# Alpha for two chunks in one transfer, two positions on a partition, in a gated linear attention with a multiplicative feed-forward

## The chip, the cores and the metric

The kernel runs on one core of a Trainium2 chip. The metric is the device time of one execution in microseconds (us); the figure used is the median of several executions. The profile is of one further execution, and its span is a little different from the median. Engines are named as in the profile: PE is TensorE's matmul, PEld its weight load, DVE is VectorE, ACT ScalarE, POOL GpSimd, SP SyncE; a name with q at its end is that engine's own queue, for instance SPq, the SyncE queue that issues most of the DMA transfers.

## What is computed

A recurrence over 768 positions for 4 x 8 heads of 48 columns, and a feed-forward block on its output. All products have to be close to float32.

```python
def _attn_ref(q, k, v, alpha):                 # (4, 8, 768, 48) each, float32
    for t in range(S):
        state = alpha[:, :, t, :, None] * state + einsum('bhd,bhde->bhde' of k, v: outer product)
        y[:, :, t] = np.einsum('bhd,bhde->bhe', q[:, :, t], state)

# bridge: (B,H,S,D) -> x of (B*S, H*D) = (3072, 384)
def _moe_ref(x, w1, w2, w3, w_out):            # weights arrive as float64
    a = x @ w1                                 # 384 x 1024
    b = x @ w2
    h = a * b @ w3                             # 1024 x 1024
    return (h @ w_out).astype(np.float32)      # 1024 x 384
```

alpha lies between 0.8 and 1.0. (The einsum of the state is written here in words; the whole is the outer product of k and v at each position.)

## The kernel before

The positions are cut in chunks of C = 128, six to a batch, N = 24 in all. Within a chunk the recurrence becomes a masked matrix product: with the running sum of log(alpha) over the chunk's positions, k is multiplied by exp(-sum) and q by exp(sum); then scores = k q, masked, times v, plus the state of the chunks before. Two neighbouring chunks (n even, n + 1) share a point of reference, so an even chunk's sums run to its end and an odd one's from its start. The running sum is a product with a triangle of ones.

One chunk of alpha comes as 128 positions on 128 partitions, with 8 heads of 48 values each, and so in pieces of 48 values:

```python
    def rows(src, n):
        b, c = divmod(n, NCH)
        return src[b, :, ds(c * C, C), :].rearrange("h p d -> p h d")

    def load_a(n):
        if n < N:
            st["a", n] = inp.tile([C, H, D], FP32, tag="ac", name="ac")
            nc.sync.dma_start(out=st["a", n], in_=rows(alpha, n))           # L124
    # load_kq(n): k and q in the same way (L130, L131); load_v(n): v (L136)

    nc.scalar.preload_act_table_set(LN_EXP_SET)
    load_a(0)
    load_kq(0)
    load_a(1)
    load_v(0)
    load_kq(1)
    load_a(2)
    # ... constants: utri (ones on and above the diagonal), after = utri - 1,
    #     sums: both as fp32r
```

The logarithms, the sums and the exponentials. The first ten chunks use float32 products; from LATE = 10 on the logarithms are split in two fp32r parts:

```python
    def logs(n):
        a = st.pop(("a", n)).rearrange("p h d -> p (h d)")
        la = st["la", n] = work.tile([C, DM], FP32, tag="la", name="la")
        nc.scalar.activation(la, a, AF.Ln)                                  # L246
        if n >= LATE:
            t = st["la", n] = work.tile([C, 2, DM], FP32R, tag="la2", name="la2", bufs=1)
            nc.scalar.copy(t[:, 0], la)                                     # L250
            nc.vector.tensor_sub(t[:, 1], la, t[:, 0].bitcast(FP32))        # L251
        if n in ends:
            nc.gpsimd.dma_start(out=ends[n][2:3], in_=a[0:1])

    def decays(n):
        lc = bank()[:, 0:DM]                                                # one of 8 PSUM banks
        la = st.pop(("la", n))
        if n < LATE:
            nc.tensor.matmul(lc, utri if n % 2 else after, la, start=True, stop=True)     # L261
        else:
            for i in range(2):
                nc.tensor.matmul(lc, sums[:, n % 2], la[:, i], start=(i == 0), stop=(i == 1))  # L264
        e = st["e", n] = work.tile([C, 2, DM], FP32, tag="e", name="e", bufs=3)
        nc.scalar.activation(e[:, 0], lc, AF.Exp, scale=-1.0)               # L267
        nc.scalar.activation(e[:, 1], lc, AF.Exp)                           # L268
        if n in ends:
            nc.gpsimd.dma_start(out=ends[n][0:1], in_=e[0:1, 0])            # L270
        if n + 1 in ends:
            nc.gpsimd.dma_start(out=ends[n + 1][1:2], in_=e[C - 1:C, 1])    # L272
        load_ends(n)      # ends back from DRAM, one value to a partition, as dec (L285)

    def decayed(n):       # k and q times their exponentials
        nc.vector.tensor_mul(qks[n % 3][:, :, :, 0:D], st.pop(("kq", n)), ...)    # L277
```

What follows for a chunk: `transposed` (L299 on TensorE, copied out at L301), `scores` (L339, masked at L342), `outer` (L311), `advance` (the state times dec, L328 to L330, on GpSimd), `attend_state` (L358) and `attend` (L364, copied out at L368 and stored to DRAM by L236). Beside this the kernel converts the float64 weights (loads L181, ScalarE L189, L194, L207, VectorE L190 to L210, in steps called `convert`), and runs a part of the feed-forward's first two products as `gate` pieces (TensorE L396 and L400, emptied at L398 and L401). A gate product takes three fp32r parts of each operand, so that the result is as good as float32.

The order of the work:

```python
    logs(0)
    decays(0)
    decayed(0)
    transposed(0)
    logs(1)
    decays(1)
    convert(1, 1)
    load_v(1)
    load_kq(2)
    load_a(3)
    # ... decayed(1), further loads, load_a(4)

    for n in range(N + 1):
        store()
        load_v(n + AHEAD - 1)
        load_a(n + 5)
        load_kq(n + AHEAD)
        # attend_state(n - 1), scores(n), transposed(n + 1), split_x
        pieces = (0, 3, 3, 2)[(n - 6) % 4] if n > 5 else 0
        if n == 0:
            logs(2)
            decays(2)
            logs(3)
        # convert, advance(n), attend(n - 1), outer(n)
        run(pieces > 0)                     # gate pieces
        decayed(n + 2)
        logs(n + 4)
        # load_x, convert
        run(pieces > 1)
        decays(n + 3)
        # convert
        run(pieces > 2)
```

After the loop come the rest of the weights, w3 and w_out folded to one matrix (L439, L445), the other gate products, and the last product with the folded matrix (L396 and L400 with other tiles).

Of the kernel before, what the change touches and what calls it, by code (L numbers as in the profile page):

```python
# [10 lines left out]
FP32 = mybir.dt.float32  # L11
FP32R = mybir.dt.float32r
# [3 lines left out]
AF = mybir.ActivationFunctionType  # L16
ALU = mybir.AluOpType
# [31 lines left out]
def kernel(  # L49
# [12 lines left out]
    nc = tc.nc  # L62
    B, H, S, D = q.shape
    C = 128
    DM = H * D
    DF = moe_w1.shape[1]
    NCH = S // C
    N = B * NCH
    NP = H // 2
    DP = 64  # L70
# [7 lines left out]
    LATE = 10  # L78
# [3 lines left out]
    def pool(name, bufs, stack=ctx, **kw):  # L82
        return stack.enter_context(tc.tile_pool(name=name, bufs=bufs, **kw))
# [13 lines left out]
    p1 = pool("p1", 1, stack=part1, side="right", reuse_waits="tile")  # L97
    inp = pool("inp", 3, stack=part1, side="right", reuse_waits="tile")
    work = pool("work", 2, stack=part1, side="right", reuse_waits="tile")

    def bank():
        return ps.tile([C, 512], FP32, tag="bank", name="bank")

    st = {}
# [4 lines left out]
    ends = {n: dram.tile([3, DM], FP32, name=f"ends{n}") for n in range(2, N, 2) if n % NCH}  # L109
# [7 lines left out]
    def rows(src, n):  # L117
        b, c = divmod(n, NCH)
        return src[b, :, ds(c * C, C), :].rearrange("h p d -> p h d")

    def load_a(n):
        if n < N:
            st["a", n] = inp.tile([C, H, D], FP32, tag="ac", name="ac")
            nc.sync.dma_start(out=st["a", n], in_=rows(alpha, n))  # L124

    def load_kq(n):
        if n >= N:
            return
        st["kq", n] = inp.tile([C, 2, H, D], FP32, tag="kq", name="kq")
        nc.sync.dma_start(out=st["kq", n][:, 0], in_=rows(k, n))  # L130
        nc.sync.dma_start(out=st["kq", n][:, 1], in_=rows(q, n))  # L131

    def load_v(n):
        if n < N:
            st["v", n] = vs[n % len(vs)]
            nc.sync.dma_start(out=st["v", n][:, :, 0:D], in_=rows(v, n))  # L136

    nc.scalar.preload_act_table_set(LN_EXP_SET)
    load_a(0)
    load_kq(0)  # L140
    load_a(1)
    load_v(0)
    load_kq(1)
    load_a(2)
# [4 lines left out]

    w12 = const.tile([C, 3, 2, KM, DF], FP32R, name="w12")  # L150

    utri = p1.tile([C, C], FP32, name="utri")
    after = p1.tile([C, C], FP32, name="after")

    sums = p1.tile([C, 2, C], FP32R, name="sums")
    keep = p1.tile([C, C], I32, name="keep")
# [1 line left out]
    Ts = [p1.tile([C, NP, DP], FP32, name=f"T{i}") for i in range(2)]  # L158
    decs = [p1.tile([C, 3, NP], FP32, name=f"dec{i}") for i in range(2)]

    make_upper_triangular(nc, utri, val=1.0, diag=True)

    nc.vector.tensor_scalar_add(after, utri, -1.0)
    nc.gpsimd.tensor_copy(out=sums[:, 0], in_=after)
    nc.gpsimd.tensor_copy(out=sums[:, 1], in_=utri)
    nc.vector.memset(rebias, -(1023.0 - 127.0) * 2.0 ** 23)

    nc.vector.tensor_scalar_mul(keep, utri, -1.0)
# [45 lines left out]
    def convert(steps, ahead=3):  # L214

        for _ in range(steps):
            while weights and len(begun) < ahead:
                begun.append(weights.popleft())
                next(begun[-1])
            if not begun:  # L220
                return
            x = begun.popleft()
            try:
                next(x)
                begun.appendleft(x)
            except StopIteration:
                pass
# [4 lines left out]
    def store():  # L232

        while later:
            dst, src = later.popleft()
            nc.sync.dma_start(out=dst, in_=src)  # L236
# [1 line left out]
    def last(n):  # L238
        return n % NCH == NCH - 1

    def logs(n):
        if n >= N:
            return
        a = st.pop(("a", n)).rearrange("p h d -> p (h d)")
        la = st["la", n] = work.tile([C, DM], FP32, tag="la", name="la")
        nc.scalar.activation(la, a, AF.Ln)  # L246
        if n >= LATE:

            t = st["la", n] = work.tile([C, 2, DM], FP32R, tag="la2", name="la2", bufs=1)
            nc.scalar.copy(t[:, 0], la)  # L250
            nc.vector.tensor_sub(t[:, 1], la, t[:, 0].bitcast(FP32))  # L251
        if n in ends:
            nc.gpsimd.dma_start(out=ends[n][2:3], in_=a[0:1])

    def decays(n):
        if n >= N:
            return
        lc = bank()[:, 0:DM]
        la = st.pop(("la", n))
        if n < LATE:  # L260
            nc.tensor.matmul(lc, utri if n % 2 else after, la, start=True, stop=True)  # L261
        else:
            for i in range(2):
                nc.tensor.matmul(lc, sums[:, n % 2], la[:, i], start=(i == 0), stop=(i == 1))  # L264

        e = st["e", n] = work.tile([C, 2, DM], FP32, tag="e", name="e", bufs=3)
        nc.scalar.activation(e[:, 0], lc, AF.Exp, scale=-1.0)  # L267
        nc.scalar.activation(e[:, 1], lc, AF.Exp)  # L268
        if n in ends:
            nc.gpsimd.dma_start(out=ends[n][0:1], in_=e[0:1, 0])  # L270
        if n + 1 in ends:
            nc.gpsimd.dma_start(out=ends[n + 1][1:2], in_=e[C - 1:C, 1])  # L272
        load_ends(n)

    def decayed(n):
        if n < N:
            nc.vector.tensor_mul(qks[n % 3][:, :, :, 0:D], st.pop(("kq", n)),  # L277
                                 st.pop(("e", n)).rearrange("p i (h d) -> p i h d", h=H))

    def load_ends(n):  # L280
        if n not in ends:
            return
        with nc.allow_non_contiguous_dma(reason="single values to partitions"):
            for i in range(2):
                nc.gpsimd.dma_start(out=decs[n // 2 % 2][ds(DP * i, D)].rearrange("d m j -> d (m j)"),  # L285
                                    in_=ends[n].rearrange("m (j i d) -> i d (m j)", i=2, d=D)[i])

    def transposed(n):
        if n >= N:
            return  # L290
        qk = qks[n % 3]
        qkT = work.tile([C, 2, NP, C], FP32, tag="qkT", name="qkT")

        tp = [bank().rearrange("p (i j c) -> p i j c", i=2, j=NP) for _ in range(2)]
        for i in range(2):
            for j in range(NP):
                for half in range(2):
                    s = ds(DP * half, DP)
                    nc.tensor.transpose(tp[half][:, i, j, :], qk[s, i, 2 * j:2 * j + 2, :], ident[s, s])  # L299
        for half in range(2):  # L300
            nc.scalar.copy(qkT[:, :, :, ds(DP * half, DP)], tp[half])  # L301
        st["qkT", n] = qkT
# [44 lines left out]
    def attend_state(n):  # L347
        qkT = st.pop(("qkT", n))

        y = [bank()[:, 0:HP * C].rearrange("p (j c) -> p j c", c=C) for _ in range(2)]
        st["y", n] = y, [(half * HP + j, i, y[i][ds(DP * half, DP), j, :])
                         for j in range(HP) for i in range(2) for half in range(2)]
        if n % NCH:
            for j, i, to in st["y", n][1]:
                r = ds(DP * i, D)
                nc.tensor.matmul(to, Ts[n % 2][r, j, :], qkT[r, 1, j, :],  # L358
                                 start=(j % HP == 0), stop=False, skip_group_check=True)
# [115 lines left out]
    fill = deque()  # L475

    def run(pieces):

        for _ in range(pieces):
            if not fill:  # L480
                return
            try:
                next(fill[0])
            except StopIteration:
                fill.popleft()
# [3 lines left out]
        for kk in range(KM):  # L489
            weights.append(load_gates(kk, c0, CW // 2))  # L490

    logs(0)
    decays(0)
    decayed(0)
    transposed(0)
    logs(1)
    decays(1)
    convert(1, 1)
    load_v(1)
    load_kq(2)  # L500
    load_a(3)
    decayed(1)
    load_v(2)
    load_kq(3)
# [5 lines left out]
# [5 lines that stand above are left out]
        if n:  # L515
            attend_state(n - 1)
        if n < N:
            scores(n)
        transposed(n + 1)
        if n - 2 in begin:  # L520
            g, tiles = begin[n - 2]
            split_x(g, 0)
            fill.extend(gate(g, f) for f in tiles)
        pieces = (0, 3, 3, 2)[(n - 6) % 4] if n > 5 else 0
        if n == 0:
            logs(2)
            decays(2)
            logs(3)
        early = n < 7
        convert(1, 2 if n == 0 else 3)  # L530
        advance(n)
        if n:
            attend(n - 1)
        outer(n)
        run(pieces > 0)
        if early:
            convert(1)
        decayed(n + 2)
        logs(n + 4)
        if n in begin:  # L540
            load_x(begin[n][0])
        convert(early and n > 2)
        run(pieces > 1)
        decays(n + 3)
        convert(early or n % 3 == 0)
        run(pieces > 2)
# [82 lines left out]
```

## Time and profile before

| | |
|---|---|
| device time, median of 3 | 491.05 us (490.73 to 491.96) |
| span of the profiled execution | 492.8 us |
| TensorE busy | 462.0 us, 94% |
| VectorE busy | 371.0 us, 75% |
| ScalarE busy | 250.1 us, 51% |
| alpha's transfers | 24, 192 KB each, median 5.0 us from issue to landing |
| Ln of one chunk (L246) | 24, mean 529 ns |
| sums, float32 (L261) | 10 and 10 instructions, mean 683 and 616 ns |
| sums, fp32r (L264) | 28, mean 350 ns |

A float32 product shows as two TensorE instructions, a fp32r product as one. The mean of a TensorE instruction is its time through the engine; instructions that follow one another overlap, so the time that a row of them takes is less than the count times the mean. In the page's second part the span is cut in 40 slices of 12.3 us, and each digit is the busy share in tenths. The chain of waits goes back from the last instruction to what released it, and is best read in order of time.

### The profile page before, as it was taken

How to read it: one execution, taken by the hardware profiler on the slowest of the kernel's cores; microseconds unless marked ns; L12 is line 12 of the kernel's file. 1: busy time of each engine (PE TensorE's matmuls, PEld its weight loads, DVE VectorE, ACT ScalarE, POOL GpSimd, SP SyncE). 2: the span in 40 equal slices, each digit the busy share in tenths (PEclk: the TensorE clock that was granted, in tenths of full speed). 3: DMA queues.
4: the chain of work that ended last, by engine and by line, in shares of the span. 5: the costliest groups of instructions: out<-in, count | busy, mean ns of one | idle time of the engine just before them, and what ended most of it. 6: DMA issues, size and time to landing. Idle time of an engine off the chain costs nothing.

```text
span 492.8 us, 9909 instructions
## 1 busy us (share of the span) xinstructions
PE 462.0 (94%) x3760; PEld 422.5 (86%) x3760; DVE 371.0 (75%) x620; ACT 250.1 (51%) x479; POOL 37.5 (8%) x83
## 2 busy tenths in 40 slices
PE   3788689999998979999999999999999999999997
PEld 1566479888998968999999988888888999999996
DVE  2779899887988684999999769686433786667771
ACT  2767677676765563555556444444222533333330
POOL 2132132021103100000000000000000000000000
PEclk9989999999999998999999999999999999999999
DMA  9999999899999963666454433320001875555511
GB/s 176 185 200 205 236 199 201 217 183 234 194 227 189 214 207 101 175 183 195 158 195 155 156 117 118 118 92 32 33 32 61 229 225 176 177 176 178 176 49 48
DMA packets 160495, 79.10 MB, mean 161 GB/s; under 512 B 104640, under 2 KB 154304, under 8 KB 160448
## 3 DMA queue, kind: packets, MB, share of 16 engines
q1 hardware_dynamic: 159168, 78.40, 62.7%
q0 software_dynamic: 1280, 0.08, 0.4%
q8 instruction: 29, 0.48, 0.4%
q14 instruction: 18, 0.15, 0.1%
HBM read 56.40 MB, written 22.06 MB: 159 GB/s over the span
## 4 chain that ended last, share of the span: by engine, by line
PE 73%; DVE 9%; DMA 8%; SPq 4%; issue 3%; ACT 2%; POOL 0%; DVEq 0%; POOLq 0%; ACTq 0%
PE bank L396 37%; PE bank L400 18%; PE bank L445 8%; DMA raw<-in_moe_w_dram 3%; PE bank L339 2%; PE bank L364 2%; DVE ms L342 2%; PE bank L439 1%; DMA xT<-xd 1%; DMA abd<-ab 1%; DMA dec<-ends 1%; PE bank L299 1%; SPq L130 1%; DVE qk L277 1%; SPq L124 1%
## 5 line engine op out<-in xcount | busy, mean ns | idle before, releaser
L396 PE MATMUL bank<-x,w 128*128 128x384 f32 x768 | 159.3, 341 | 0.0
L396 PEld LDWEIGHTS bank<-x,w 128*128 128x128 f32 x768 | 134.6, 188 | 3.5 <-issue 0.5
L398 ACT ACTIVATE t<-bank 128x384 f32<-128x384 f32 x152 | 74.5, 492 | 109.7 <-PE bank L396 97.8
L401 DVE SCALAR_TENSOR_TENSOR r<-bank,t 128x384 f32<-128x384 f32 x128 | 69.7, 555 | 34.0 <-ACT t L398 32.1
L400 PE MATMUL bank<-x,w 128*128 128x384 f32 x384 | 87.3, 335 | 0.4 <-DVE x L387 0.4
L396 PE MATMUL bank<-w3o,ab 128*128 128x384 f32 x384 | 70.4, 334 | 0.0
L400 PEld LDWEIGHTS bank<-x,w 128*128 128x128 f32 x384 | 68.3, 188 | 0.7 <-issue 0.7
L396 PEld LDWEIGHTS bank<-w3o,ab 128*128 128x128 f32 x384 | 66.9, 188 | 0.0
L445 PE MATMUL bank<-wo,w3T 128*128 128x384 f32 x128 | 42.6, 486 | 0.0
L189 ACT ACTIVATE rest<-raw 128x512 f32<-128x512 uint32 (+1 forms) x36 | 23.4, 651 | 33.0 <-DMA raw<-in_moe_w_dram 20.5
L412 DVE TENSOR_TENSOR ab<-r 128x384 f32<-128x384 f32 x64 | 35.6, 556 | 2.3 <-DMA abd<-ab 1.5
L400 PE MATMUL bank<-w3o,ab 128*128 128x384 f32 x192 | 37.1, 334 | 0.0
L445 PEld LDWEIGHTS bank<-wo,w3T 128*128 128x128 f32 x128 | 24.2, 189 | 14.9
L464 DVE TENSOR_TENSOR ab<-abl,ab 128x1024 fp32r<-128x1024 f32 x24 | 29.4, 1224 | 9.2 <-ACT ab L463 9.2
L339 PEld LDWEIGHTS bank<-qkT 48*128 48x128 f32 x384 | 25.4, 200 | 12.4 <-ACT qkT L301 5.7
L339 PE MATMUL bank<-qkT 48*128 48x128 f32 x384 | 30.3, 299 | 6.0 <-ACT qkT L301 4.3
L463 ACT ACTIVATE ab<-abl 128x1024 fp32r<-128x1024 f32 x24 | 25.5, 1064 | 19.0 <-PE bank L400 18.8
L400 PEld LDWEIGHTS bank<-w3o,ab 128*128 128x128 f32 x192 | 33.6, 188 | 0.0
L342 DVE TENSOR_TENSOR ms<-bank,keep 128x512 int32<-128x512 int32 x48 | 31.1, 684 | 1.7 <-PE bank L339 1.7
L194 ACT ACTIVATE power<-power,rebias 128x512 uint32<-128x512 uint32 (+1 forms) x36 | 25.3, 705 | 12.2 <-DVE power L193 12.2
L401 DVE SCALAR_TENSOR_TENSOR o<-bank,t 128x384 f32<-128x384 f32 x24 | 13.4, 557 | 22.4 <-issue 13.7
L277 DVE TENSOR_TENSOR qk<-kq,e 128x768 f32<-128x768 f32 x24 | 22.9, 953 | 9.5 <-ACT e L268 7.2
(69 smaller groups left out, 540.1 us busy)
## 6 DMA issues: line engine op xcount, KB each, us to landing
abd<-ab SPq DMA_DIRECT2D x64, 192.0 KB, 2.7
abl<-abd SPq DMA_DIRECT2D x24, 512.0 KB, 4.5
raw<-in_moe_w_dram SPq DMA_DIRECT2D x16, 512.0 KB, 3.9
xT<-xd SPq DMA_DIRECT2D x12, 576.0 KB, 4.2
raw<-in_moe_w_dram SPq DMA_DIRECT2D x24, 256.0 KB, 4.8
ac<-in_alpha_dram SPq DMA_DIRECT2D x24, 192.0 KB, 5.0
kq<-in_k_dram SPq DMA_DIRECT2D x24, 192.0 KB, 5.4
kq<-in_q_dram SPq DMA_DIRECT2D x24, 192.0 KB, 4.3
```

The source lines that it names most:

```text
L194: nc.scalar.activation(power, power, AF.Relu, scale=2.0 ** 23, bias=rebias)
L277: nc.vector.tensor_mul(qks[n % 3][:, :, :, 0:D], st.pop(("kq", n)), st.pop(("e", n)).rearrange("p i (h d) -> p i h d", h=H))
L339: nc.tensor.matmul(sc[i][:, j, :], qkT[r, 0, j, :], qkT[r, 1, j, :], start=True, stop=True)
L342: nc.vector.tensor_tensor(ms[:, i].bitcast(I32), sc[i].bitcast(I32), keep_bc, op=ALU.bitwise_and)
L396: nc.tensor.matmul(p1, w[part][i], x[part][i], start=(part == i == 0), stop=(part == 1 and i == n - 1))
L398: nc.scalar.activation(t, p1, AF.Copy, scale=(1.0 + 1.0 / P) * scale)
L400: nc.tensor.matmul(p2, w[2][i], x[2][i], start=(i == 0), stop=(i == n - 1))
L401: nc.vector.scalar_tensor_tensor(to, p2, -scale, t, op0=ALU.mult, op1=ALU.add)
L412: nc.vector.tensor_mul(ab, *r)
L445: nc.tensor.matmul(po, w3T[:, j, :], wo[:, j, :], start=(j == 0), stop=(j == KF - 1))
L463: nc.scalar.activation(t[:, 0], ab, AF.Copy, scale=1.0 - 2.0 ** -13)
L464: nc.vector.tensor_sub(t[:, 1], ab, t[:, 0].bitcast(FP32))
```

## The change

Alpha comes for two chunks (n even, n + 1) in one transfer. Two neighbouring positions lie on one partition, so partitions 0 to 63 hold chunk n and 64 to 127 chunk n + 1, and a piece is 96 values long. The sum over a chunk's 128 positions then is two products of 64 rows, one for the first positions of the pairs and one for the second; the products of the two chunks use different halves of TensorE's rows and different banks. The triangle is kept in the matching form. The purpose is fewer and longer pieces of DMA, and half as many instructions for the logarithms. At the start, the pair of chunks 0 and 1 is loaded and worked in two halves.

```diff
-    def load_a(n):
-        if n < N:
-            st["a", n] = inp.tile([C, H, D], FP32, tag="ac", name="ac")
-            nc.sync.dma_start(out=st["a", n], in_=rows(alpha, n))
+    def load_a(n, parts=(slice(0, C),)):
+
+        if n >= N or n % 2:
+            return
+        b, c = divmod(n, NCH)
+        src = alpha[b, :, ds(c * C, 2 * C), :].rearrange("h (p r) d -> p h (r d)", r=2)
+        if ("a", n) not in st:
+            st["a", n] = inp.tile([C, H, 2 * D], FP32, tag="ac", name="ac", bufs=2)
+        for r in parts:
+            nc.sync.dma_start(out=st["a", n][r], in_=src[r])
@@
-    load_a(0)
+    pair = slice(0, DP), slice(DP, C)
+    load_a(0, pair[:1])
     load_kq(0)
-    load_a(1)
+    load_a(0, pair[1:])
@@ (constants: the triangle as [64 rows x 2 chunks, 2, 128] in place of utri and after)
+    tri = work.tile([C, 2, C], FP32, tag="qkT", name="tri")
+    nc.gpsimd.memset(tri, 1.0)
+    for i in range(2):
+        for r in range(2):
+            nc.gpsimd.affine_select(out=tri[ds(DP * i, DP), r], in_=tri[ds(DP * i, DP), r], ...)
+    nc.vector.tensor_scalar_add(sums[0:DP], tri[0:DP], -1.0)
+    nc.vector.tensor_copy(out=sums[DP:], in_=tri[DP:])
@@ logs
+        if n >= N or n % 2:
+            return
+        la, = st["la", n]                       # [C, H, 2 * D]
+        for r in parts:
+            nc.scalar.activation(la[r], a[r], AF.Ln)
         if n >= LATE:
-            t = st["la", n] = work.tile([C, 2, DM], FP32R, tag="la2", name="la2", bufs=1)
+            t = work.tile([C, 2, H, 2 * D], FP32R, tag="la2", name="la2", bufs=1)
+            st["la", n] = [t[:, 0], t[:, 1]]
@@ decays
-        lc = bank()[:, 0:DM]
-        la = st.pop(("la", n))
-        if n < LATE:
-            nc.tensor.matmul(lc, utri if n % 2 else after, la, start=True, stop=True)
-        else:
-            for i in range(2):
-                nc.tensor.matmul(lc, sums[:, n % 2], la[:, i], start=(i == 0), stop=(i == 1))
+        parts = st["la", n]
+        w = sums if n >= LATE else sums.bitcast(FP32)
+        lc = {i: bank()[:, 0:DM] for i in chunks}
+        for x in parts:
+            for r in range(2):
+                for i in chunks:
+                    half = ds(DP * i, DP)
+                    nc.tensor.matmul(lc[i].rearrange("p (h d) -> p h d", h=H), w[half, r], x[half, :, ds(r * D, D)],
+                                     start=(x is parts[0] and r == 0), stop=(x is parts[-1] and r == 1))
+        for i in chunks:                        # the two exponentials of each chunk, and its ends, as before
@@ order
-    logs(0)
-    decays(0)
+    logs(0, pair[:1])
+    decays(0, (0,))
     decayed(0)
     transposed(0)
-    logs(1)
-    decays(1)
+    logs(0, pair[1:])
+    decays(0, (1,))
     convert(1, 1)
     load_v(1)
     load_kq(2)
-    load_a(3)
@@ in the loop
         if n == 0:
             logs(2)
             decays(2)
-            logs(3)
```

The loop's calls are the same; those of load_a, logs and decays with an odd n now do nothing, and those with an even n serve both chunks.

More of the change, by code (lines that the diff above doesn't have):

```diff
@@ L150 @@
     w12 = const.tile([C, 3, 2, KM, DF], FP32R, name="w12")
-    utri = p1.tile([C, C], FP32, name="utri")
-    after = p1.tile([C, C], FP32, name="after")
     sums = p1.tile([C, 2, C], FP32R, name="sums")
@@ L159 @@
     decs = [p1.tile([C, 3, NP], FP32, name=f"dec{i}") for i in range(2)]
+    utri = work.tile([C, C], FP32, tag="x", name="utri")
     make_upper_triangular(nc, utri, val=1.0, diag=True)
-    nc.vector.tensor_scalar_add(after, utri, -1.0)
-    nc.gpsimd.tensor_copy(out=sums[:, 0], in_=after)
-    nc.gpsimd.tensor_copy(out=sums[:, 1], in_=utri)
+    tri = work.tile([C, 2, C], FP32, tag="qkT", name="tri")
+    nc.gpsimd.memset(tri, 1.0)
+    for i in range(2):
+        for r in range(2):
+            nc.gpsimd.affine_select(out=tri[ds(DP * i, DP), r], in_=tri[ds(DP * i, DP), r], compare_op=ALU.is_ge, fill=0.0,
+                                    base=-r, pattern=[[1, C]], channel_multiplier=-2)
+    nc.vector.tensor_scalar_add(sums[0:DP], tri[0:DP], -1.0)
+    nc.vector.tensor_copy(out=sums[DP:], in_=tri[DP:])
     nc.vector.memset(rebias, -(1023.0 - 127.0) * 2.0 ** 23)
@@ L239, in last, with logs @@
         return n % NCH == NCH - 1
-    def logs(n):
-        if n >= N:
+    def logs(n, parts=(slice(0, C),)):
+        if n >= N or n % 2:
             return
-        a = st.pop(("a", n)).rearrange("p h d -> p (h d)")
-        la = st["la", n] = work.tile([C, DM], FP32, tag="la", name="la")
-        nc.scalar.activation(la, a, AF.Ln)
+        a = st["a", n]
+        if ("la", n) not in st:
+            st["la", n] = [work.tile([C, H, 2 * D], FP32, tag="la", name="la", bufs=1)]
+        la, = st["la", n]
+        for r in parts:
+            nc.scalar.activation(la[r], a[r], AF.Ln)
         if n >= LATE:
-            t = st["la", n] = work.tile([C, 2, DM], FP32R, tag="la2", name="la2", bufs=1)
+            t = work.tile([C, 2, H, 2 * D], FP32R, tag="la2", name="la2", bufs=1)
+            st["la", n] = [t[:, 0], t[:, 1]]
             nc.scalar.copy(t[:, 0], la)
@@ L252, in logs, with decays @@
         if n in ends:
-            nc.gpsimd.dma_start(out=ends[n][2:3], in_=a[0:1])
-    def decays(n):
-        if n >= N:
+            nc.gpsimd.dma_start(out=ends[n][2:3].rearrange("m (h d) -> m h d", h=H), in_=a[0:1, :, 0:D])
+    def decays(n, chunks=(0, 1)):
+        if n >= N or n % 2:
             return
-        lc = bank()[:, 0:DM]
-        la = st.pop(("la", n))
-        if n < LATE:
-            nc.tensor.matmul(lc, utri if n % 2 else after, la, start=True, stop=True)
-        else:
-            for i in range(2):
-                nc.tensor.matmul(lc, sums[:, n % 2], la[:, i], start=(i == 0), stop=(i == 1))
[L266 to L273, printed above, removed]
+        parts = st["la", n]
[8 more added lines that the diff above has]
+        for i in chunks:
+            e = st["e", n + i] = work.tile([C, 2, DM], FP32, tag="e", name="e", bufs=3)
+            nc.scalar.activation(e[:, 0], lc[i], AF.Exp, scale=-1.0)
+            nc.scalar.activation(e[:, 1], lc[i], AF.Exp)
+            if n + i in ends:
+                nc.gpsimd.dma_start(out=ends[n][0:1], in_=e[0:1, 0])
+                load_ends(n)
+            if n + i + 1 in ends:
+                nc.gpsimd.dma_start(out=ends[n + 2][1:2], in_=e[C - 1:C, 1])
     def decayed(n):
```

## The prediction

> **What bounds the kernel now.** I read the page's busy rows first, then its slices, then the busy time by stretches, then the chain of waits.
>
> ```profile
> span 492.8 us, 9909 instructions
> PE 462.0 (94%) x3760; PEld 422.5 (86%) x3760; DVE 371.0 (75%) x620; ACT 250.1 (51%) x479; POOL 37.5 (8%) x83
> PE   3788689999998979999999999999999999999997
> ...
> DMA  9999999899999963666454433320001875555511
> DMA packets 160495, 79.10 MB, mean 161 GB/s; under 512 B 104640, under 2 KB 154304, under 8 KB 160448
> ```
>
> TensorE is busy for 462.0 of 492.8 us, so all the time that any change can win without taking TensorE work away is 30.8 us. The slices say where it lies: the first six have the low digits, while the DMA row is full for about the first 15 slices (185 us). That is the stage the change touches; all its loads are over by 154 us, as the view of alpha's tile shows. The same by stretches (columns: us, then busy us of TensorE, weight loads, VectorE, ScalarE, GpSimd, granted clock, DMA share, GB/s):
>
> ```profile
> 0.00:6.00 6.00, 1.65 (x2) 0.50 (x2) 1.67 (x6) 1.81 (x2) 2.85 (x19) 1.00 0.80 139
> 6.00:12.00 6.00, 2.63 (x18) 1.46 (x18) 0.96 (x1) 1.81 (x4) 0.60 (x1) 1.00 1.33 208
> 12.00:18.00 6.00, 2.97 (x34) 2.79 (x33) 3.53 (x7) 3.01 (x6) 0.58 (x2) 1.00 1.24 193
> ...
> 42.00:48.00 6.00, 5.68 (x98) 4.44 (x97) 6.00 (x12) 4.74 (x11) 1.45 (x3) 1.00 0.94 224
> ...
> 70.00:80.00 10.00, 10.00 (x137) 9.29 (x131) 10.00 (x21) 7.88 (x18) 1.73 (x4) 1.00 0.91 184
> ```
>
> Adding the rows up to 60 us gives TensorE 40.8 us busy, 19.2 idle. From 60 to 190 us it idles some 8 us, in the last stage 3.9. From 42 us on VectorE is as full as TensorE (the conversion of the weights). So three resources run side by side: DMA over the whole stage, VectorE from 42 to 100 us, TensorE from 70 us. Saved DMA time becomes saved time only where TensorE stands: mostly in the head.
>
> The chain in the head, in order of time (start, us, what):
>
> ```profile
> 6.48 1.10 SPq L124
> ...
> 8.68 4.65 DMA raw<-in_moe_w_dram
> ...
> 15.10 2.08 PE bank L339 x16
> 18.03 1.21 PE bank L261 x2
> 20.04 3.77 DMA ends<-e
> 25.14 5.69 DMA dec<-ends
> ```
>
> The SyncE queue issues loads one after another for 8.6 us; then the first weights arrive; ScalarE, which takes its work in order, stands before their conversion (L189) with the copies of the transposes (L301) behind it; then scores, decays, and two small transfers that carry the chunk's decay.
>
> **What the Trainium skill says.** DMA: Bandwidth & Descriptors, Specifications: transfers want 512 B or more for line rate. The trace agrees in direction: its packet records have 98304 packets of 192 B at a mean of 18.4 ns and 33792 of 512 B at 29.5 ns, so 2.7 times the bytes cost 1.6 times the time. TensorEngine Tiling (Array Packing), Key Properties: row tiles can load weights and multiply in parallel, but a change of tiling mode drains the engine. Both are visible. A 384-column float32 instruction takes 5.16/16 = 0.322 us in a full row (L445), so 128 columns take 0.107 us, and sixteen in series 1.72 us; the sixteen of L339, on alternating halves of the rows, take 1.09 to 1.16 us. And 13 times a weight load of L358, which follows in another mode, waits on "issue" for 5.5 us in all. Same page, Gotcha 1: PSUM Pressure: the two row tiles must write different banks; the changed code gives each chunk its own.
>
> **The change part by part.**
>
> *Alpha's transfers.* Before: 24 transfers of 8 x 128 packets of 192 B, 24576 packets. After: 12288 packets of 384 B. Before they cost 24576 x 18.4 ns / 16 = 28.3 us of all engines. For 384 B I interpolate between the two measured sizes: 18.4 + (192/320) x 11.1 = 25 ns, so 19.2 us. Saved: 9.1 us of DMA time, spread over some 155 us, 6% of the stage. In the first 60 us alpha is loaded for about 10 chunks: 10/24 x 9.1 = 3.8 us of DMA. In issue slots, L124 has a median of 0.81 us and 12 issues of 24 go away (the prologue's one pair in two halves brings one back).
>
> *Prologue, what goes.* Of eight transfers ahead of the first weights, each of 1024 packets, two now have 512: one packet block less, about 0.9 us earlier. On ScalarE the copies of chunk 0's transposes now stand ahead of the first conversion. Before they ran at 13.98 us although the transposes ended at 10.5; after, I put them at about 11 us. Up to 3 us of that waiting ends.
>
> *Prologue, what comes.* Each chunk's sum is now two float32 products, four instructions, not two. There the two took 1.65 us, so four take about 3 us: 1.3 us more, twice, in a row that nothing overlaps. Ln for a chunk is 64x768 for 128x384: from 529 ns (384 columns) and 1167 ns (1152 columns, L385), 0.83 ns a column, so 848 ns: 0.3 us more, twice. Following it through: first exponentials at 7.7 (before 7.4), transposes 9.7 to 10.8, second sum to 13.7, scores to 15.7 (before 17.2), second chunk's transposes to 17 (before 18), then the pair's sums, exponentials of chunk 2 at 19 to 20 (before 19.3). So the 3 us are mostly eaten by the 2.6 + 0.6 us of added work: net about 0.
>
> *The sums later.* Float32 (n < 10): per pair eight instructions in the order half 0, 0, half 1, 1. Alternation allows five slots of 0.322 us, against four before: +0.3 us a pair, less one start-up of about 0.27 us: even. From chunk 10, 28 fp32r products of 128 rows become 56 of 64, strictly alternating. One takes 2.77/16 = 0.173 us; side by side 28 slots as before. Two mode changes a pair at 0.1 to 0.5 us for those seven: +1 to 2 us at the most. TensorE's sum stays within 2 us.
>
> *ScalarE and VectorE.* Ln: 24 x 529 = 12.7 us becomes about 12 x 848 = 10.2. Copy to fp32r 7.2 becomes 7 x 830 = 5.8. Subtraction on VectorE: 14 x 554 = 7.8 becomes 7 x 953 = 6.7, with L277's 768 columns as measure. VectorE wins 1.1 us, of which the head, where it binds, gets little, as chunks before 10 have no subtraction.
>
> *Moves.* The second chunk's sum comes an iteration early, so its exponentials are ready earlier; logs have a whole iteration of lead for both. The four waits of L277 on e (7.2 us) and those of L261 on la (8.6 us) lie almost wholly in the head. Against this, four exponentials come in a row, 4 x 0.49 = 2 us, and may delay an emptying of a bank.
>
> *Sum.* Prologue 0. Loads of the weights earlier in the DMA-full stretch from 20 to 42 us: two issues and 1.5 to 1.9 us of DMA fewer ahead of them at 22 us, of which VectorE, idle 3.6 us from 24 to 36, can use about 1.5 to 2. The 8 us of waits from 60 to 190: DMA load 6% lighter, 1 to 2 us. Mode changes and bursts: -1. Together about 3 us: 491.05 - 3 = 488.0 us.
>
> **The rivals.**
>
> *A: DMA sets the pace of the whole stage,* and 9 us come off it. For it: the full DMA row and a SyncE queue that issues almost without a gap from 20 to 80 us, some issues stretched to 3.9 us. Against it: TensorE is busy all 10 us of most stretches from 70 us on, with work that the change doesn't remove. It would make 481 to 484 us.
>
> *B: The halves don't run side by side,* or drain each time. 28 x 0.173 = 4.8 us more from chunk 10 on, and some 10 x 0.645 = 6.5 us in the head, half of it beside idle time: 494 to 499 us. L339 and the transposes speak against it; no fp32r product on half the rows is in this trace.
>
> *C: The added float32 products delay the head.* The first exponentials, then chunk 2's decay, whose two transfers end the wait at 31 us, come later by 1 to 3 us: 490 to 493 us.
>
> **Range and chances.** The middle is the sum. A lends the lower end, weakened since TensorE caps it: 483.5. C and a part of B lend the upper: 494. Faster by over 2% means under 481.2, which takes a third of all idle time: 0.05. Slower by over 2% means over 500.9, more than B's whole: 0.03. The rest, 0.92, is within 2%.
>
> **What would show it.** Right: alpha's packets of 384 B near 25 ns; TensorE's busy time within 2 us of 462; copies of the first transposes near 11 us; the first gate product (L396 before) starting 1 to 3 us earlier than 62.6 us, where it starts now, and the rest shifted by as much. Wrong: a pair's eight fp32r products taking about 1.5 us and not 0.8 (B); the first gate product later (C); TensorE idle from 60 to 190 us falling to nothing and the head shorter by 6 us or more (A).

## The result, and the profile after

The changed kernel is slower, by a little: 495.58 us (495.47 to 496.2, 4 runs) against 491.28 us (490.73 to 491.96, 4 runs), a ratio of 1.0089 [1.0072, 1.0107]. Repeated later on one chip beside the experiments it was 497.43 us against 494.35 us, 1.0063 [1.004, 1.0085]. Predicted were 488.0 us and a range up to 494.0.

The page's busy rows and slices after:

```profile
span 494.5 us, 9992 instructions
PE 464.9 (94%) x3808; PEld 423.9 (86%) x3808; DVE 370.0 (75%) x614; ACT 247.8 (50%) x461; POOL 40.0 (8%) x86
PE   3969779999999999999999999999999999999996
...
DMA packets 148032, 79.12 MB, mean 160 GB/s; under 512 B 92176, under 2 KB 141840, under 8 KB 147984
```

12464 packets under 512 B are gone, and the engines' busy times have moved little (TensorE's by 2.9 us). The profiled execution of the kernel before took 494.63 us, 3.3 more than its median, so the two traces differ by less than the medians do; I read places from them, and sums from the timed runs. The stretches (columns as before: us, busy of TensorE, weight loads, VectorE, ScalarE, GpSimd, granted clock, DMA share, GB/s):

```profile
6.00:12.00 6.00, 3.77 (x21) 2.05 (x20) 0.96 (x1) 2.08 (x4) 0.00 (x0) 1.00 1.36 211
12.00:18.00 6.00, 5.75 (x38) 4.41 (x38) 3.53 (x7) 4.14 (x9) 1.24 (x2) 1.00 1.39 211
...
70.00:80.00 10.00, 8.82 (x100) 7.03 (x101) 8.63 (x15) 7.02 (x15) 1.29 (x4) 0.83 1.00 225
```

From 6 to 18 us TensorE is busy for 9.5 us, where it was busy for 5.6: the sums for the most part (the first starts 1.0 us later, and each takes longer), and scores that come earlier. From 70 to 80 us it is no longer full, and its granted clock is 0.83, not 1.00. The chain of waits in the head (start, us, what):

```profile
10.51 1.12 PE bank L319 x16
11.63 1.39 PE bank L282 x2
...
17.37 2.91 PE bank L282 x8
20.28 0.48 ACT e L287
21.04 4.49 DMA ends<-e
...
26.85 6.77 DMA dec<-ends
```

The scores of chunk 0 no longer wait for the weights' conversion. In their place the sums (L282) are on the chain, and the decay's two transfers start 1.0 and 1.7 us later than before and take 0.7 and 1.1 us longer. TensorE's waits (total, times, longest):

```profile
PE bank L378 <- POOL T L350: 5.4, 2, 4.7
...
PE bank L282 <- ACT la L266: 1.7, 1, 1.7
PE bank L420 <- ACT qkT L321: 1.2, 1, 1.2
```

The wait for the state (T, which waits for the decay) has grown from 2.2 to 5.4 us. The last two rows, small as they look, mark the other places of the loss. Taking the start of each chunk's scores as milestones: chunk 7 begins 2.0 us later than before (60.01 against 58.02), chunk 8 5.9 us later (76.31 against 70.38), chunk 21 3.9 (174.83 against 170.91), chunk 22 5.4 (183.32 against 177.92). So in this pair of traces time is lost in the head, in the step from chunk 7 to 8, and in the step from 21 to 22; in between some is won back. Chunk 23 then begins only 3.0 us later (188.28 against 185.25), in part because the kernel before runs at half clock from 186.0 to 189.4 us, in its step from 22 to 23.

**The step from 7 to 8** holds the first pair in fp32r, chunks 10 and 11. The kernel before, by the timeline:

```profile
66.16 0.49 ACT L398 ACTIVATE t<-bank 128x384 f32<-128x384 f32 x1 [0.54 <-PE bank L396]
...
66.55 0.52 ACT L246 ACTIVATE la<-ac 128x384 f32<-128x384 f32 x1
...
67.10 0.51 ACT L250 CAST la<-la 128x384 fp32r<-128x384 f32 x1
...
67.66 0.44 PE L264 MATMUL bank<-la,sums 128*128 128x384 f32 x1 [1.01 <-ACT la L250]
```

And the changed kernel:

```profile
69.04 0.49 ACT L418 ACTIVATE t<-bank 128x384 f32<-128x384 f32 x1 [0.58 <-PE bank L416]
...
69.43 0.83 ACT L261 ACTIVATE la<-ac 128x768 f32<-128x768 f32 x1
...
70.29 0.83 ACT L266 CAST la<-la 128x768 fp32r<-128x768 f32 x1
...
71.18 0.62 PE L282 MATMUL bank<-la,sums 64*128 64x384 f32 x4 [1.65 <-ACT la L266]
...
72.94 1.01 PE L282 MATMUL bank<-la,sums 64*128 64x384 f32 x4
```

In both, the logarithm stands on ScalarE behind the emptying of a gate bank, and TensorE waits for logarithm and copy to pass. They are now for two chunks, 0.83 + 0.83 us, not 0.52 + 0.51, and the wait is 1.65, not 1.01 us. The data can't be the reason: this alpha was issued at 56.81 us, and no load of alpha between 35 and 95 us took over 7.7 us. The place in ScalarE's row is. The eight products also come in two groups of four with gate products between them, so TensorE changes its mode four times, where one group of eight would need two. Then this (the same columns as the stretches above):

```profile
72.20:75.60 3.40, 3.40 (x12) 2.26 (x10) 2.73 (x5) 1.62 (x5) 0.53 (x1) 0.50 1.02 272
```

The clock is halved for 3.4 us, which takes 1.7 us if all of it is TensorE's work, as here. With it the 3.9 us by which the step is longer come out nearly: 0.6 us from the wait for the copy, 1.7 from the clock, 1.0 from the wait for chunk 8's k and q (2.28 us, before 1.28); the sums of chunk 11 are done in this step too. The Trainium skill (TensorE: Matmul & The Clock Gate, Part 1: The HAM clock gate) has a half rate after an idle window of about 3.4 us, and windows that run free. The trace agrees on the rate and on the length; it shows no idle time of 3.4 us ahead, only TensorE busy for 8.0 of 12.2 us from 60 to 72.2.

**The step from 21 to 22.** ScalarE in the changed kernel:

```profile
180.91 0.55 ACT L200 ACTIVATE rest<-raw 128x384 f32<-128x384 uint32 x1 [3.87 <-DMA raw<-in_moe_w_out_dram]
181.35 1.06 ACT L321 COPY qkT<-bank 128x512 f32<-128x512 f32 x2
...
181.98 0.79 PE L420 MATMUL bank<-x,w 128*128 128x384 f32 x3 [1.19 <-ACT qkT L321]
```

The copies of chunk 22's transposes stand behind a conversion of w_out whose load comes late. The kernel before has the same neighbourhood:

```profile
174.75 0.56 ACT L189 ACTIVATE rest<-raw 128x384 f32<-128x384 uint32 x1 [4.35 <-DMA raw<-in_moe_w_out_dram]
175.21 1.06 ACT L301 COPY qkT<-bank 128x512 f32<-128x512 f32 x2
```

There it is the first conversion of five in this stretch, 3.8 us after chunk 21's scores; now it is the fifth, 6.1 us after them, and TensorE has run out of other work. No line of the change touches this; the order on an in-order engine was put together anew.

### The profile page after: what moved, and what is told of

It reads as the page before. It is cut to its first block, busy times and chain, and to the rows that moved or that the text cites. A ratio compares the mean times of both kernels' runs of the same rounds, so it can differ in the third digit from the quotient of the medians.

```text
span 494.5 us, 9992 instructions
## 1 busy us (share of the span) xinstructions
PE 464.9 (94%) x3808; PEld 423.9 (86%) x3808; DVE 370.0 (75%) x614; ACT 247.8 (50%) x461; POOL 40.0 (8%) x86
## 4 chain that ended last, share of the span: by engine, by line
PE 78%; DVE 8%; DMA 7%; ACT 3%; issue 2%; SPq 1%; POOL 0%; DVEq 0%; POOLq 0%; ACTq 0%
PE bank L416 40%; PE bank L420 19%; PE bank L465 8%; PE bank L359 2%; PE bank L384 2%; PE bank L282 2%; DMA raw<-in_moe_w_out_dram 2%; PE bank L459 1%; DMA dec<-ends 1%; PE bank L319 1%; DVE ms L362 1%; DVE qk L297 1%; DMA ac<-in_alpha_dram 1%; DMA ends<-e 1%; PE bank L378 1%
## 5 line engine op out<-in xcount | busy, mean ns | idle before, releaser
L321 ACT COPY qkT<-bank 128x512 f32<-128x512 f32 x48 | 25.8, 590 | 16.0 <-PE bank L319 16.0
```

## The experiments

Three explanations stood at first: the head through the decay's transfers (rival C), the form of the sums from chunk 10 on, and longer pieces that gain nothing. Rows with the same time before were on the same chip beside it. Every time depends on the granted clock of its run; in each group a straight line with a common slope (-297 to -322 us per unit of mean clock) fits this, and the last column is the difference to the kernel before at equal clock, in us, with 95%. The ratio and the last column leave out the few executions in the chip's slower state. The ratio is the record's own estimate and not the quotient of the medians (for pairs_from2 that would be 1.0038, and for early_load10 1.0005). Equal clock has a weakness: the clock isn't chance alone. Over all its executions after_no_ends had a mean of 0.989 and before_no_ends of 0.984, so what a kernel does to the clock is taken out of its difference. Where the medians say something else, both are given.

| run | us | before | ratio [95%] | at equal clock |
|---|---|---|---|---|
| late_pairs | 495.93 | 492.77 | 1.0082 [1.0056, 1.0108] | +3.1 ± 0.9 |
| early_pairs | 493.57 | 492.77 | 1.0017 [0.9985, 1.005] | +0.3 ± 0.8 |
| pairs_from4 | 495.41 | 492.77 | 1.005 [1.0024, 1.0075] | +3.1 ± 1.1 |
| pairs_from2 | 494.63 | 492.77 | 1.0006 [0.9981, 1.003] | +1.0 ± 0.7 |
| after_again | 497.43 | 494.35 | 1.0063 [1.004, 1.0085] | +3.5 ± 0.6 |
| before_no_ends | 491.98 | 494.35 | 0.9958 [0.9933, 0.9982] | -2.1 ± 0.6 |
| after_no_ends | 493.14 | 494.35 | 0.9977 [0.9957, 0.9997] | +0.6 ± 0.6 |
| short_pieces | 500.55 | 494.35 | 1.0119 [1.0081, 1.0157] | +6.7 ± 1.0 |
| after_late12 | 495.4 | 493.55 | 1.0038 [1.0007, 1.007] | +3.3 ± 0.8 |
| before_late12 | 493.7 | 493.55 | 1.0005 [0.9977, 1.0033] | +0.1 ± 0.7 |
| early_load10 | 493.79 | 493.55 | 1.0012 [0.9992, 1.0032] | +0.8 ± 0.6 |
| from2_early10 | 491.46 | 493.55 | 0.9962 [0.9941, 0.9983] | -1.7 ± 0.6 |
| before_early10 | 495.76 | 494.42 | 1.0024 [0.9998, 1.0049] | -0.1 ± 0.7 |
| from4_early10 | 493.26 | 494.42 | 0.9987 [0.9964, 1.001] | +0.2 ± 0.7 |

### Which chunks cost: the pair form for a part of them

Four kernels use the pair form for some chunks only and the old form for the others:

```diff
+def PAIRED(n):
+    return n >= 10      # late_pairs; early_pairs: n < 10; pairs_from4: n >= 4; pairs_from2: n >= 2
@@ load_a, logs, decays
+        if n < N and not PAIRED(n - n % 2):
+            ...         # as in the kernel before, in the halves of the pair's tiles
@@ late_pairs and early_pairs: the triangle of the other form is written on GpSimd at n = 7
```

> Chunks 0 to 9 one by one as in the kernel before, pairs only from chunk 10 on (the triangle is rewritten on GpSimd in between). Theory head (the loss lies in the first 65 us: chunk 2's exponentials come 1 us later, its two small decay transfers take 1.8 us longer, TensorE stands 4.7 us instead of 2.2 before the first product with the state): 489.5 to 491.5, as the kernel before or a little less. Rival stage (four exponentials in a row, mode changes and the larger loads cost time in every pair): 494 to 495.5.

> Pairs for chunks 0 to 9, one by one from chunk 10 on. Theory head: 494.5 to 496, as the changed kernel. Rival stage: 491.5 to 493, as only five of twelve pairs are left.

> Chunks 0 to 3 one by one, pairs from chunk 4 on. Theory head: 489.5 to 491.5, as nothing ahead of chunk 2's decay is changed. Rival stage: 494 to 495.5.

> Chunks 0 and 1 one by one, pairs from chunk 2 on: tells the doubled float32 products of the first two chunks from the pair of chunks 2 and 3. Theory head by the prologue's added products: 490.5 to 492.5. Theory head by the pair 2 and 3 (eight cold float32 instructions ahead of chunk 2's exponentials) or by the earlier weight loads that collide with the decay transfers: 494 to 496. Rival stage: 494 to 495.5.

Pairs from chunk 10 on alone cost about as much as the whole change, and pairs up to chunk 9 alone can't be told from the kernel before. late_pairs, early_pairs and pairs_from4 all came out in the range of the rival stage or within 0.6 us of it, so the theory that the loss lies in the head fell. A second trace agrees: in after_again chunk 7 begins at 57.81 us, no later than in the kernel before (58.02), so the 2.0 us of the first trace aren't steady. Yet the two chunks of the prologue matter by themselves: with only those two back in the old form (load, logarithms and sums together) +1.0 us is left of +3.5. TensorE's row in the head shows what that takes away. The changed kernel:

```profile
5.35 2.92 PE L282 MATMUL bank<-la,sums 64*128 64x384 f32 x4 [5.35 <-ACT la L261]
...
13.56 2.44 PE L359 MATMUL bank<-qkT 48*128 48x128 f32 x13
```

And pairs_from2 (its L309 are the old sums, L409 the scores):

```profile
4.47 1.65 PE L309 MATMUL bank<-la,sums 128*128 128x384 f32 x2 [4.47 <-ACT la L277]
...
12.12 2.08 PE L409 MATMUL bank<-qkT 48*128 48x128 f32 x16
```

A prologue sum takes 1.65 us, not 2.92, and chunk 0's scores are through at 14.2, not at 16.0 us. The pair's eight products follow at 16.20 and not at 17.30, and TensorE's wait for the state falls to 2.66 us from 4.75.

pairs_from4 is a surprise: putting chunks 2 and 3 back too costs 2 us more again (2.1 ± 1.1 at equal clock, 0.8 in the medians). ScalarE's row shows why. In pairs_from4 the copies of chunk 0's transposes (L371) stand behind the first conversion of the weights (L218), as in the kernel before:

```profile
13.83 0.69 ACT L218 ACTIVATE rest<-raw 128x512 f32<-128x512 uint32 x1 [5.35 <-DMA raw<-in_moe_w_dram]
14.40 1.06 ACT L371 COPY qkT<-bank 128x512 f32<-128x512 f32 x2
...
15.52 2.08 PE L409 MATMUL bank<-qkT 48*128 48x128 f32 x16 [3.21 <-ACT qkT L371]
```

In pairs_from2 they stand ahead of it:

```profile
10.62 1.07 ACT L371 COPY qkT<-bank 128x512 f32<-128x512 f32 x2 [2.26 <-PE bank L369]
```

So pairs_from2 keeps what the change won on ScalarE and drops what the added sums cost. Chunk 3's scores start at 33.68 us in it and at 35.20 in pairs_from4. The same holds with the earlier load below: 33.79 in from2_early10, 35.25 in from4_early10.

### The decay's transfers, and the longer pieces

```diff
@@ before_no_ends, after_no_ends: no decay at all; the state is multiplied by zero in its place
-        if n in ends:
-            nc.gpsimd.dma_start(out=ends[n][2:3], in_=a[0:1])
@@ (and the two of decays; load_ends returns at once)
```

> The changed kernel once more, unaltered, beside more executions of the kernel before: 494.5 to 496.5 if the 4 us are a property of the kernel. If they were largely the chance of few executions (the kernel before spread over 8 us in the earlier comparison), 492.5 to 494.5, within 2 us of the kernel before.

> The kernel before without the small transfers of the decay at the chunks' ends (it leaves out the decay of the state between pairs of chunks: the state is multiplied by zero). Theory head (the wait for the decay transfers): TensorE's wait of 2.2 us at 32 us goes, 488 to 490. If these waits are hidden elsewhere, 490.5 to 492.5.

> The changed kernel with the same omission. Theory head: the wait of 4.7 us goes, the distance to the other kernel without these transfers falls from 4 us to under 1 us. Rival stage or products: the distance stays at 3 to 4 us.

after_again is 3.1 us slower than the kernel before beside it, so the loss belongs to the kernel and not to a few executions. The other two leave out the transfers that carry a chunk's decay, and so compute something else. If the change lost its time through these transfers alone, the two should be equal. Their distance is 1.2 us in the medians, 2.8 ± 0.7 us at equal clock, where it was 3.1 and 3.5 with the transfers. By the medians the transfers would explain up to 1.9 us of the loss, at equal clock 0.7 us; these two runs don't decide how much. That they aren't the main cause rests on late_pairs, which leaves the head as it was and loses as much.

```diff
@@ short_pieces: the changed kernel, pieces of 48 values as before
-            nc.sync.dma_start(out=st["a", n][r], in_=src[r])
+            for i in range(2):
+                nc.sync.dma_start(out=st["a", n][r, :, ds(D * i, D)], in_=src[r, :, ds(D * i, D)])
```

> The changed kernel, but each pair of alpha comes by two transfers in pieces of 192 B, as many packets and transfers as in the kernel before; the rest is as changed. If the longer pieces bring DMA time that counts: 1 to 3 us slower than the changed kernel, 496 to 498. If DMA isn't what ends last: the same within 1 us.

500.55 against 497.43 us: the longer pieces and fewer issues are worth 3.1 us (3.2 ± 1.0 at equal clock). They do gain. But short_pieces isn't the kernel before in this respect: it splits each half of the first pair once more, and so has six issues of alpha ahead of the first weights, where the kernel before has three. Its first sum starts at 6.37 us, not at 5.35, and chunk 3's scores at 37.23, not at 35.94. So about 1 us of the 3.2 is its own head (an estimate from these starts), and the rest of the change costs between 5.7 and 6.7 us.

### From chunk 10 on: the place of the logarithms

```diff
@@ after_late12, before_late12: chunks 10 and 11 by float32 products, without the copy to fp32r
-    LATE = 10
+    LATE = 12
@@ early_load10: alpha from pair 10 on one pass of the loop earlier
-        load_a(n + 5)
+        load_a(n + 5 if n < 4 else n + 6)
@@ from2_early10: early_load10 with chunks 0 and 1 in the old form (pairs_from2)
```

> The changed kernel with float32 sums up to chunk 11 (LATE = 12), so that chunk 10's pair, the first at which TensorE has gate products to do, has no split into fp32r parts between its logarithms and its sums. Theory first split pair (TensorE waits there 1.65 us, or 2.45 us with pairs from chunk 10 only, for 0.83 us of Ln and 0.83 us of copy for two chunks, and often drops to half clock after it): 2 to 3 us faster than the changed kernel although it has some 0.9 us more products. Rival products (the doubled products of the first chunks and mode changes, in TensorE's own busy time): the same as the changed kernel or 1 us slower.

> The control: the kernel before with LATE = 12. Both theories: within 1 us of the kernel before, as its wait at that place is 1.0 us and the added products are 2 x 0.3 us.

> The changed kernel, but from chunk 10 on a pair of alpha is loaded one iteration earlier; with it the logarithms and the copy of chunk 10's pair stand ahead of the first gate product's emptying on ScalarE. Theory first split pair: 2 to 3 us faster than the changed kernel, the wait for the copy at about 70 us gone. Rival products: the same as the changed kernel.

> Chunks 0 and 1 one by one, pairs from chunk 2 on, with the earlier loads from chunk 10 on: takes away the doubled products of the first two chunks and the wait at the first split pair together. If both are what the change costs and the longer pieces bring 3 us (by the kernel with short pieces): 1 to 3 us faster than the kernel before. Otherwise within 1 us of the kernel before or slower.

after_late12 is a miss: I had expected 2 to 3 us, and at equal clock nothing is gained (its control before_late12 doesn't move either). Its copies for chunk 22 still stand behind a conversion that waits 3.59 us for w_out, and its step from 21 to 22 is 8.4 us, as in the changed kernel (8.5). Its step from 7 to 8 is the shortest of all kernels with pairs there, 15.0 us, and still nothing is gained, so the length of one step doesn't tell the kernel's time. early_load10, in contrast, wins 2.7 us at equal clock, by one number in a load's index. TensorE's row in it:

```profile
64.78 1.12 PE L319 MATMUL bank<-ident,qk 64*128 64x64 f32 x16 [3.75 <-DVE qk L297]
...
72.03 0.96 PE L282 MATMUL bank<-la,sums 64*128 64x384 f32 x8
```

The first fp32r pair is eight products in one group and without a wait, since its logarithm now runs at 60.80 us. But a part is given back at once: the subtraction that belongs to the pair now stands on VectorE ahead of the multiplication for chunk 8, and that wait is 3.75 us. The step from 7 to 8 falls only from 16.3 to 15.4 us (before: 12.4). The other part of the gain is where no one would look for it, at chunk 22:

```profile
177.12 1.06 ACT L321 COPY qkT<-bank 128x512 f32<-128x512 f32 x2
...
180.30 0.55 ACT L200 ACTIVATE rest<-raw 128x384 f32<-128x384 uint32 x1 [1.57 <-DMA raw<-in_moe_w_out_dram]
```

The copies now stand ahead of the conversion that waits for w_out, and TensorE doesn't wait. The step from 21 to 22 takes 7.0 us, as in the kernel before. Over the traces of all kernels this splits cleanly: where chunk 22's copies start within 5 us of chunk 21's scores the step is 7.0 us (nine traces, with the kernel before), where they start over 6 us after them it is 8.3 to 10.4 us (seven: the changed kernel twice, late_pairs, pairs_from2, short_pieces, after_late12, after_no_ends). pairs_from4 is among the nine, since its load of w_out came in time, and is slow all the same, with a step from 7 to 8 of 16.9 us. That step is 12.4 to 13.1 us wherever chunks 10 and 11 are single, and 15.0 to 17.1 us in every kernel with pairs there. A rival for a part of this is the clock: in all eleven traces with pairs there it is halved for 3.4 or 6.8 us within the step, with the earlier load too, and in the five others only in before_early10, which has the longest step of the five.

from2_early10 puts the earlier load and the old prologue together and beats both kernels: 491.46 us, 0.9962 [0.9941, 0.9983].

### What was still open: is an earlier load a gain of its own?

```diff
@@ before_early10: the kernel before, its alpha earlier in the same way
-        load_a(n + 5)
+        if n < 5:
+            load_a(n + 5)
+        if n >= 4:
+            load_a(n + 6)
@@ from4_early10: pairs_from4 with the earlier load
```

> The control to the earlier loads: the kernel before, with alpha's single chunks from 10 on loaded one iteration earlier. If the earlier load repairs something that the pairs brought: within 1 us of the kernel before. If it is a gain of its own that any version has: 2 to 3 us faster than the kernel before, 490 to 491.5 where that has 493.5.

> Chunks 0 to 3 one by one, pairs from chunk 4, loads one iteration earlier from chunk 10 on. If the costs add up (first chunks 2.5 us, late order of the logarithms 2.5 us), both are away: as the version with pairs from chunk 2 and earlier loads, 1 to 3 us faster than the kernel before. If pairs from chunk 4 have a cost of their own (without the earlier loads they were 2 us slower than pairs from chunk 2): 0 to 1 us slower than the kernel before.

In the kernel before the earlier load gains nothing (-0.1 ± 0.7 us at equal clock, 1.3 us slower in the medians). So it repairs something that the pairs brought. With pairs it is worth the same three times, each against the kernel before on its own chip: 2.7 (changed kernel), 2.7 (pairs_from2) and 2.9 us (pairs_from4). Chunks 0 and 1 in the old form are worth 2.5 us without and 2.5 us with the earlier load (each of these differences is good to 0.7 to 1.2 us). So the two costs add up. from4_early10 comes out between its two expectations (1.2 us faster than the kernel before in the medians, +0.2 ± 0.7 at equal clock) and behind from2_early10: it lacks what the pair of chunks 2 and 3 brings.

## Why the prediction was wrong

The measured account at equal clock, by blocks of chunks in the pair form: chunks 0 and 1 +2.5 us (after_again less pairs_from2), chunks 2 and 3 -2.1 (pairs_from2 less pairs_from4), chunks 4 to 9 0.0 (pairs_from4 less late_pairs), chunks 10 to 23 +3.1 (late_pairs less the kernel before), each good to about 1 us. That these add up to the measured +3.5 is so by construction; early_pairs is the test, for which they give +0.4 and which measured +0.3 ± 0.8. The gain of the longer pieces is spread over the blocks. So the head as a whole comes out even, and the loss arises from chunk 10 on, where the earlier load takes back 2.7 us.

- **"Moves" failed, and with it the forecast.** For the stage from chunk 10 on the sum had 1 to 2 us of waits won, less 1 for "mode changes and bursts"; measured were +3.1 ± 0.9. "Logs have a whole iteration of lead for both" was read from the calls in the loop. In the trace the pair's logarithm, called a pass ahead of its sum, stands on ScalarE right behind the emptying of a gate bank, 0.83 + 0.83 us ahead of the sum that waits. And nothing in the step allowed for the order changing elsewhere, as with w_out's conversion 110 us later. That the late place costs is shown by the earlier load, worth 2.7 us with pairs and nothing without; that it acts through ScalarE's order is read from the traces (the logarithm at 60.80 us, not at 69.43).
- **"Prologue 0" held as a sum.** The changed kernel is 0.4 us slower than pairs_from4, which has chunks 0 to 3 as before (0.7 us with the earlier load in both), within noise of 0. Both its parts were there too: the wait on ScalarE that ends ("Up to 3 us"), for which I take the 2.1 us that pairs in chunks 2 and 3 bring, and the added work that eats it (2.6 + 0.6 us), for which I take the 2.5 us of chunks 0 and 1. Its steps came 0.3 to 0.8 us later than said: the logarithm of the first half starts at 4.45 us and not at 3.77 as before, the first exponentials at 8.50 (7.7 said), the transposes at 10.51 (9.7 said), their copies at 11.63 (about 11 said), the scores of chunk 0 end at 16.0 (15.7 said), chunk 2's exponentials start at 20.3 (19 to 20 said). The transfers after them, which the step didn't follow further, took 1.8 us longer in sum. Rival C had its cost right, but chunks 2 and 3 bring nearly as much back, so it isn't what made the change slower.
- **"For 384 B I interpolate" was off in size.** The packets took 30.0 ns in the mean, not 25 ns, so alpha's DMA time fell from 28.3 to 12288 x 30.0 / 16 = 23.0 us: 5.3 us saved, not 9.1. The time gained by it, 3.2 us at most, is about what the sum had for loads and waits, but other costs of the pair form ate it.
- **"Loads of the weights earlier" came true and bought nothing that can be seen.** The first pair of issues came 0.4 us later (8.03 us; 0.9 earlier was said), those from 20 to 55 us came 1.1 to 2.6 us earlier (21.49 for 22.57 us, 53.07 for 55.71). TensorE's first gate product nevertheless starts at 65.56 us, not at 62.6 or earlier, and the pair form of chunks 4 to 9 measured 0.0 ± 1.3 us, where the term was 1.5 to 2 us of gain.
- **"TensorE's sum stays within 2 us" can't be judged on one trace.** It is 464.9 us, 2.9 more, but 463.4 in after_again; and before_no_ends, with the old sums, has 465.9. The granted clock moves it by as much.
- **Rival B was rightly held unlikely.** A pair's eight fp32r products without a gap, in the changed kernel:

```profile
91.27 0.96 PE L282 MATMUL bank<-la,sums 64*128 64x384 f32 x8
```

A chunk's two full-row products took 0.62 us at that point of the kernel before, and 1.5 for a pair had been named as the sign of halves in series. Rival A fell with the 5.3 us and with the first gate product.

Open ends remain. What share of the 3.1 us falls to chunk 10 and what to chunk 22 differs from trace to trace, and no run settles it: after_late12 shortens only the first of these steps, pairs_from4 only the second, and both are slow. Whether the half clock in the step from 7 to 8 is a cause or a companion isn't settled: after_again has the same wait of 1.65 us at chunk 10 and its stretch at half clock ahead of it (from 62.7 us), and its step is 15.9 us all the same. late_pairs and early_pairs rewrite the triangle on GpSimd at n = 7, which the other kernels don't, and its cost isn't measured apart. What the mode changes of the sums cost no run shows.

## What to carry to other kernels

On an in-order engine the place of an instruction is read from the trace of the built kernel, not from the order of the calls; when two chunks' work is merged into one instruction, check what stands behind it and what it stands behind, also far from the change, and try moving its load by one pass before giving the change up. A head that comes out even can hide a cost and a gain that can be had apart: here the pair form cost 2.5 us in chunks 0 and 1 and gained 2.1 in chunks 2 and 3, and a merged form may start two chunks later and keep the gain. With that and the earlier load from2_early10 is 0.9962 of the kernel before, with the same idea that gave 1.0063. And when a variant puts old code back, read in its trace which order came back with it.

## What the runs showed of the hardware

Pieces of 384 B cost 30.0 ns a packet and those of 512 B 29.9 ns in the changed kernel's trace (28.8 and 29.9 in after_again's), so the time between 192 B (18.4 ns) and 512 B isn't a straight line. The granted clock of TensorE falls to 0.5 for 3.4 or 6.8 us at a time, once 10.2, and not by the length of one wait alone: in short_pieces it falls at 130.4 us where no wait in the 5.4 us ahead was over 1.27 us (TensorE busy for 3.12 of them), and in the kernel before a wait of 2.19 us at 50.0 us is not followed by a fall. Such stretches differ from execution to execution of one kernel: 10.2 us in the changed kernel's trace, 6.8 in after_again's. The runs of the kernel before on one chip spread from 490.4 to 497.9 us, and follow the mean clock at some 300 us per unit.
